# The remainder rows of a down product: one product of 96 rows, or three rounds of 32-row products in four row groups

## The chip, the cores and the metric

The kernel runs on one core of one Trainium2 chip. The metric is the device time of one execution in microseconds (us). One core has TensorE (PE, matrix products; its weight loads are listed apart as PEld), VectorE (DVE), ScalarE (ACT), GpSimd (POOL) and SyncE (SP, which here issues DMAs). Each engine works through its own instructions in order and waits on semaphores for the others.

## The reference

```python
def _B_ref(x, w_gate, w_up, w_down):
    return (_gelu(x @ w_gate) * (x @ w_up)) @ w_down
...
x = A_x
xn = _layernorm(x, axis=-1)
return x + _A_ref(xn, ...) + _B_ref(xn, B_w_gate, B_w_up, B_w_down)
```

`x` is 2048 tokens of 512 features in bfloat16. `_B_ref` is a gated feed-forward layer with an inner width of F = 1376. `_A_ref` is a state-space layer: each of 512 complex states is decayed from token to token and takes an input from a product with `B_re + iB_im`; the states are multiplied by `C_re + iC_im`, the real part doubled, and `xn * Dskip` added.

1376 = 10 x 128 + 96. The inner width is thus ten full tiles of 128 rows and a remainder of 96. This remainder is the subject here.

## The kernel before

**Blocks and stages.** The 2048 tokens are four blocks of 512 (b = 0 to 3), each of four token tiles of 128 (j). For a block there are: normalisation; a transposition to feature-major (XNT); `BU`, 32 products that give the inputs of the states, followed by `CHAIN` on VectorE (a rotation, eight scans over the 512 tokens, a rotation back) which leaves the states in SS; `GU`, the gate and up products for row tiles ft = 0 to 10 of the inner width, which after gelu on ScalarE and a multiply on VectorE leave the tile HT[b % 2][ft] (128 inner rows x 512 tokens); and `DN`, the down product, which sums in a PSUM bank, for each token tile, the products of HT with WD (11 row tiles) and of SS with CT (8 products), and puts out the sum with the skip terms.

**The down product (DN, L847 to L884).** Line 857 has the products over HT, line 865 those over SS, line 876 the product of the remainder where it is done late. Each has a token tile of 128 as its weights and 512 output features as its columns. The remainder's tile HT[.][10] holds 96 rows; it is padded with zeros to 128, as is WD's, by memsets on GpSimd at the start (L515, L516), so the remainder is one product of 128 rows per token tile. After a tile's products, `skip` (L843 to L845) prepares x + xn * Dskip on VectorE, `evO` (L881) adds it to the PSUM bank and writes OUTB, and SyncE stores it (L883).

**The remainder rows of HT.** The up products of the remainder are packed: for all blocks `GU_rest` (L801) computes the 96 gate columns and 32 of the up columns in one set of four products (L808), and `UP_rest` (L825) computes the other 64 up columns for two blocks at a time, side by side in the two column halves of the array (L832), copied out by ScalarE (L838). `h_rest` (L820, its multiply is L822) then writes the 96 rows of HT[.][10]. For blocks 0 and 1 `h_rest` can only come after `UP_rest`, for blocks 2 and 3 it comes right after `GU_rest`.

**The order.** TensorE and SyncE execute in the order in which the program is written. VectorE, ScalarE and GpSimd are ordered by a planner (`Sched.schedule`), which gives each operation a due time from that of its users and its own estimated duration; a DMA has an estimated issue time (460 ns) and latency (1900 ns). All data lie in one arena with fixed places; PSUM has 8 banks, given out in turn by `next_bank`. The end of the program's order on TensorE:

```python
        def among(free):
            BU(2, banks=free + free)
            CHAIN(2)
            for i, ft in enumerate((0, 1, 2, 3, -1, 4, 5)):
                ...
        DN(0, (0, 1, 2, 3), later=among)
        GU(2, range(6, KF))
        DN(1, (0, 1, 2, 3))
        BU(3)
        CHAIN(3)
        GU(3, [KF - 1] + list(range(KF - 1)))
        DN(2, (0, 1, 2, 3))
        DN(3, (0, 1, 2))
        DN(3, (3,), 0, 384)
        DN(3, (3,), 384, 512)
```

(In `among`, -1 stands for UP_rest, the others for gu_mm and gu_out of block 2.) With `later`, DN(0) does its ten full row tiles and the SS products of all four token tiles, then `among` on the other four banks, then the four remainder products (L876). The last token tile is split into 384 and 128 columns, so that the last store is small. Products by their lines: L719 is BU, L776 gate and up, L808 GU_rest, L832 UP_rest, L857, L865 and L876 DN. VectorE by its lines: L747, L748, L749, L752 rotations, L758 scans, L768 the last step of a chain, L788 the multiply of a full row tile. CTM is a buffer that `scale_C` uses while it makes CT; the last operations that read it end before DN(0).

Of the kernel before, what the change touches and what calls it, by code (L numbers as in the profile page):

```python
# [9 lines left out]
ALU = mybir.AluOpType  # L10
# [47 lines left out]

class Op:
    __slots__ = ("id", "eng", "fn", "dur", "deps", "kind", "reads", "writes", "prio", "start", "finish",  # L60
                 "sem", "val", "users", "tag", "slack", "silent", "pin", "issue", "lat")

    def __init__(self, id_, eng, fn, dur, kind, reads, writes, tag):
        self.id, self.eng, self.fn, self.dur, self.kind = id_, eng, fn, float(dur), kind
        self.reads, self.writes, self.tag = reads, writes, tag
        self.deps, self.users = [], []
        self.prio = 0.0
        self.start = self.finish = None
        self.sem = None
        self.val = None  # L70
        self.slack = 0.0
        self.pin = None
        self.silent = False
        self.issue, self.lat = 460.0, 1900.0


class Sched:
# [42 lines left out]
        return self._add(eng, fn, dur, "eng", reads, writes, tag, after)  # L120

    def dma(self, fn, nbytes, reads=(), writes=(), tag="", after=(), is_output=False, queue="sync", issue=460.0,
            lat=1900.0):
        op = self._add(queue, fn, lat + nbytes / 0.33e3, "dma", reads, writes, tag, after)
        op.issue, op.lat = issue, lat
        if is_output:
            self.out_ops.append(op)
        return op
# [113 lines left out]
    def emit(self):  # L242
# [8 lines left out]
        for e in ENGINES:  # L251
            for op in order[e]:
                if op.silent:
                    op.sem, op.val = None, 0
                elif op.kind == "eng":
                    cnt[e] += 1
                    op.sem, op.val = esem[e], cnt[e]
                else:
                    op.sem, op.val = es.enter_context(nc.semaphore("d%d" % nd)), 16
                    nd += 1  # L260
        self.n_sems = len(esem) + nd
        plan = {}
# [23 lines left out]
        for e in ENGINES:  # L286
            h = getattr(nc, e)
            for waits, op in plan[e]:
                for (s, v) in waits:
                    h.wait_ge(s, v)  # L290
                ins = op.fn(h)
                if not op.silent:
                    ins.then_inc(op.sem, 1 if op.kind == "eng" else 16)
        for (s, v) in final_waits:
            nc.sync.wait_ge(s, v)

# [16 lines left out]
def d_dve_tt2x(n): return 85.0 + 0.535 * n  # L313
def d_dve_1x(n): return 100.0 + 1.07 * n
# [6 lines left out]
def build(nc, ins, out):  # L321
    with ExitStack() as es:
# [111 lines left out]
        HT = ring(HT_all, "HT", 2)  # L434
        HTt = [[A.sub(HT[k], "HT%d_%d" % (k, ft), ft) for ft in range(KF)] for k in range(2)]
        CTM_all = A.alloc("CTM", [2, D], F32)
        CTM = ring(CTM_all, "CTM", 2)
        SSs = [[A.sub(SSb[k], "SS%d_%d" % (k, s), s) for s in range(KP)] for k in range(3)]
        SSc = [[[A.sub(SSs[k][s], "SS%d_%d_%d" % (k, s, c), c) for c in range(2)] for s in range(KP)] for k in range(3)]
# [61 lines left out]
        def late_loads():  # L501
# [12 lines left out]
              POOL(lambda e: e.iota(IOTJ.ap, [[1, 512]], base=0, channel_multiplier=0), 600, [], [IOTJ], "iotj"),  # L514
# [10 lines left out]
        def next_bank():  # L525
            b_ = rstate["n"] % 8
            rstate["n"] += 1
            return b_
# [156 lines left out]
        def factor():  # L685
# [16 lines left out]
            tt(CR, pa(NRE), pa(RDEN), ALU.mult, [PA[NRE], PA[RDEN]])  # L702
            tt(CI, pa(NIM), pa(RDEN), ALU.mult, [PA[NIM], PA[RDEN]])

        def scale_C():
            for s in range(KP):
                for c, (si, sr, op) in enumerate(((CI, CR, ALU.subtract), (CR, CI, ALU.add))):
                    m = CTM[c]
                    ACT(lambda e, s=s, si=si, m=m: e.activation(m.ap, CTR[1].ap[:, s, :], ACTF.Copy, scale=PA[si].ap[:, s:s + 1]),  # L709
                        d_act(512, 1), [CTR[1], PA[si]], [m], "cmul")  # L710
                    V(lambda e, s=s, sr=sr, m=m, op=op, c=c: e.scalar_tensor_tensor(  # L711
                        CT[c][s].ap, CTR[0].ap[:, s, :], PA[sr].ap[:, s:s + 1], m.ap, ALU.mult, op),
                      d_dve_1x(512), [CTR[0], PA[sr], m], [CT[c][s]], "cadd")

        def bu_mm(b, s, c, bank, c0, c1, toks):
            def f(e):
# [103 lines left out]
        def h_rest(b):  # L820
            ht = HTt[b % 2][KF - 1]
            V(lambda e: e.tensor_tensor(ht.ap[0:96, :], GGX[b % 2].ap[0:96, :], UPX[b].ap[0:96, :], ALU.mult),  # L822
              d_dve_tt2x(512), [GGX[b % 2]] + UPXp[b] + UPXj[b], [ht], "hmul")

        def UP_rest(banks):  # L825
            f0 = 128 * (KF - 1)
# [20 lines left out]
        def DN(b, js, c0=0, c1=512, later=None):  # L847
            k2, k3 = b % 2, b % 3
            banks = [next_bank() for _ in js]
            first = range(KF) if later is None else range(KF - 1)  # L850
            outs = [PS[bank][:, 0:c1 - c0] for bank in banks]
            parts = [bank_part(bank, 0, 4 * (c1 - c0)) for bank in banks]
            for j, o_, part in zip(js, outs, parts):
                def ffn(e, o_=o_, tok=slice(128 * j, 128 * (j + 1))):
                    ins_ = None
                    for ft in first:
                        ins_ = e.matmul(o_, HTt[k2][ft].ap[:, tok], WD.ap[:, ft, c0:c1], start=(ft == 0), stop=False)  # L857
                    return ins_
                PE(ffn, d_pe([c1 - c0] * len(first)), [HTt[k2][ft] for ft in first] + WDc, [part], "DN%d" % b)
            for j, o_, part in zip(js, outs, parts):  # L860
                def ssm(e, o_=o_, tok=slice(128 * j, 128 * (j + 1))):
                    ins_ = None
                    for s in range(KP):
                        for c in range(2):
                            ins_ = e.matmul(o_, SSc[k3][s][c].ap[:, tok], CT[c][s].ap[:, c0:c1], start=False,  # L865
                                            stop=(later is None and s == KP - 1 and c == 1))
                    return ins_
                PE(ssm, d_pe([c1 - c0] * 8), [SSs[k3][s] for s in range(KP)] + [CT[c][s] for c in range(2) for s in range(KP)],
                   [part], "DN%d" % b)
            if later is not None:  # L870
                later([bank for bank in range(8) if bank not in banks])
            for j, o_, part in zip(js, outs, parts):
                tt = 4 * b + j
                ko = tt % 4
                if later is not None:
                    PE(lambda e, o_=o_, tok=slice(128 * j, 128 * (j + 1)): e.matmul(  # L876
                        o_, HTt[k2][KF - 1].ap[:, tok], WD.ap[:, KF - 1, c0:c1], start=False, stop=True),
                       d_pe([c1 - c0]), [HTt[k2][KF - 1]] + WDc, [part], "DN%d" % b)
                if c0 == 0:
                    skip(tt)  # L880
                V(lambda e, o_=o_, ko=ko: e.tensor_tensor(OUTB[ko].ap[:, c0:c1], o_, XD[ko].ap[:, c0:c1], ALU.add),  # L881
                  d_dve_1x(c1 - c0), [part, XD[ko]], [out_part(ko, c0, c1)], "evO")
                S.dma(lambda e, tt=tt, ko=ko: e.dma_start(out[0, 128 * tt:128 * (tt + 1), c0:c1], OUTB[ko].ap[:, c0:c1]),  # L883
                      256 * (c1 - c0), reads=[out_part(ko, c0, c1)], is_output=True, tag="st_out")  # L884

        ONES = nc.const_aps.tensor(1.0, (128, 512), BF16)

# [89 lines left out]
        DN(3, (3,), 384, 512)  # L977

        S.schedule()
        S.emit()  # L980
# [54 lines left out]
```

## Time and profile before

| | us |
|---|---|
| median of 3 runs | 177.70 |
| lowest and highest run | 177.57, 177.71 |
| the profiled execution | 177.75 |
| its span, from the first to the last instruction | 176.4 |
| TensorE busy in it | 173.8 |
| VectorE busy | 161.2 |
| ScalarE busy | 102.4 |

The granted clock of TensorE is 1.000 on the mean over the span. Times in the views count from the start of the span. A product of 128 x 128 weights and 512 columns has a duration of 379 ns in the groups, but products overlap, so the chain of waits, which lists how long a row of them took, shows the pace. The trace lacks a few product records.

### The profile page before, as it was taken

What the parts mean: (1) busy time and instruction counts of PE and PEld (TensorE: products, weight loads), DVE (VectorE), ACT (ScalarE), POOL (GpSimd) and SP (SyncE); (2) the same over time, 40 slices, a digit from 0 to 9 for tenths busy, and PEclk for the clock granted to TensorE, in tenths of its full rate; (3) what the DMA queues carried; (4) which work ended last, traced back from release to release, by engine and by line L of the source; (5) the groups of instructions that cost most, each with busy time, mean ns of one, the idle gap of its engine ahead of it and who ended that gap; (6) DMA issues with size and microseconds to landing.
All of it is one profiled execution on the core that took longest, in us unless ns stands there. A gap on an engine that the chain in (4) does not pass through costs nothing.

```text
span 176.4 us, 2434 instructions
## 1 busy us (share of the span) xinstructions
PE 173.8 (99%) x889; PEld 82.3 (47%) x889; DVE 161.2 (91%) x251; ACT 102.4 (58%) x194; POOL 14.3 (8%) x25
## 2 busy tenths in 40 slices
PE   8999999999999999999999999999999999999995
PEld 2784444444444444444444444444444444444454
DVE  5889999998999999999899999899989999999831
ACT  3599999889999995866785700026866620000000
POOL 5130110000033019000000000000000000000000
DMA  5999825986000041230003000120000000002111
GB/s 153 252 243 342 246 59 98 320 173 186 0 0 0 4 87 33 58 61 0 4 2 119 0 0 0 35 89 0 0 0 0 4 0 0 0 0 78 45 59 59
DMA packets 26345, 12.38 MB, mean 70 GB/s; under 512 B 17662, under 2 KB 26334, under 8 KB 26334
## 3 DMA queue, kind: packets, MB, share of 16 engines
q1 hardware_dynamic: 25270, 11.71, 26.2%
q10 hardware_dynamic: 1064, 0.53, 1.0%
q8 instruction: 7, 0.11, 0.3%
q14 instruction: 4, 0.03, 0.1%
HBM read 6.46 MB, written 2.10 MB: 49 GB/s over the span
## 4 chain that ended last, share of the span: by engine, by line
PE 99%; DVE 0%; issue 0%
PE PS L776 38%; PE PS L857 21%; PE PS L865 16%; PE PS L719 16%; PE PS L892 3%; PE PS L808 2%; PE PS L613 2%; PE PS L832 1%; PE PS L589 1%; PE PS L876 0%; DVE arena L881 0%; PE PS L622 0%
## 5 line engine op out<-in xcount | busy, mean ns | idle before, releaser
L776 PE MATMUL PS<-arena 128*128 128x512 bf16 (+2 forms) x328 | 68.0, 366 | 0.0
L776 PEld LDWEIGHTS PS<-arena 128*128 128x128 bf16 x328 | 31.2, 98 | 35.2 <-ACT arena L838 0.4
L758 DVE TENSOR_TENSOR_SCAN arena<-arena 128x512 bf16<-128x512 f32 x32 | 38.4, 1252 | 0.0
L857 PE MATMUL PS<-arena 128*128 128x512 bf16 (+2 forms) x183 | 38.1, 366 | 0.0
L865 PE MATMUL PS<-arena 128*128 128x512 bf16 (+2 forms) x136 | 28.6, 366 | 0.0
L719 PE MATMUL PS<-arena 128*128 128x512 bf16 x128 | 28.3, 379 | 0.0
L784 ACT ACTIVATE arena<-PS 128x512 bf16<-128x512 f32 x40 | 23.8, 596 | 6.4 <-PE PS L776 4.9
L857 PEld LDWEIGHTS PS<-arena 128*128 128x128 bf16 x183 | 17.6, 98 | 19.9
L728 ACT ACTIVATE arena<-PS 128x512 bf16<-128x512 f32 x26 | 15.2, 600 | 19.9 <-PE PS L719 19.7
L786 ACT ACTIVATE arena<-PS 128x512 bf16<-128x512 f32 x40 | 23.9, 598 | 4.7 <-PE PS L776 4.5
L865 PEld LDWEIGHTS PS<-arena 128*128 128x128 bf16 x136 | 13.0, 98 | 14.7
L719 PEld LDWEIGHTS PS<-arena 128*128 128x128 bf16 x128 | 12.5, 98 | 14.9
L747 DVE TENSOR_TENSOR arena<-arena 128x4096 bf16<-128x4096 bf16 x8 | 18.3, 2286 | 0.1
L748 DVE TENSOR_TENSOR arena<-arena 128x4096 bf16<-128x4096 bf16 x8 | 18.3, 2284 | 0.0
L788 DVE TENSOR_TENSOR arena<-arena 128x512 bf16<-128x512 bf16 x40 | 16.0, 418 | 2.0 <-ACT arena L786 1.7
L881 DVE TENSOR_TENSOR arena<-PS,arena 128x512 bf16<-128x512 f32 (+2 forms) x17 | 10.7, 652 | 6.6 <-PE PS L865 5.8
L845 DVE TENSOR_TENSOR arena<-arena 128x512 f32<-128x512 bf16 x16 | 10.6, 689 | 0.4
L749 DVE TENSOR_TENSOR arena<-arena 128x2048 bf16<-128x2048 bf16 x8 | 9.8, 1222 | 0.2
L637 ACT ACTIVATE arena<-arena 128x512 bf16<-128x512 bf16 x8 | 5.8, 800 | 2.6 <-POOL arena L630 2.6
L534 DVE BATCH_NORM_STATS2 arena<-arena 128x6 f32<-128x512 bf16 x8 | 5.2, 680 | 1.5 <-DMA arena<-in_A_x_dram 1.4
L844 DVE TENSOR_TENSOR arena<-arena 128x512 bf16<-128x512 bf16 x16 | 6.3, 418 | 0.0
L711 DVE SCALAR_TENSOR_TENSOR arena<-arena 128x512 bf16<-128x512 bf16 x8 | 5.7, 747 | 0.5 <-ACT arena L709 0.5
(78 smaller groups left out, 113.3 us busy)
## 6 DMA issues: line engine op xcount, KB each, us to landing
out_dram<-arena SPq DMA_DIRECT2D x15, 128.0 KB, 1.7
arena<-in_A_x_dram SPq DMA_DIRECT2D x3, 512.0 KB, 6.8
arena<-in_B_w_down_dram SPq DMA_DIRECT2D x1, 1280.0 KB, 7.7
arena<-in_B_w_gate_dram SPq DMA_DIRECT2D x2, 384.0 KB, 6.5
arena<-in_B_w_up_dram SPq DMA_DIRECT2D x2, 384.0 KB, 7.0
arena<-in_A_x_dram SPq DMA_DIRECT2D x4, 128.0 KB, 3.1
arena<-in_B_w_gate_dram ACTq DMA_DIRECT2D x1, 256.0 KB, 3.2
arena<-in_B_w_up_dram ACTq DMA_DIRECT2D x1, 256.0 KB, 4.0
```

The lines of the kernel that those rows point to most:

```text
L719: ins_ = e.matmul(PS[bank][:, c0:c1], BBT[c].ap[:, dk, 128 * s:128 * (s + 1)], XNT[b].ap[:, dk, c0:c1], start=(dk == 0), stop=(dk == KD - 1))
L728: return ACT(lambda e: e.activation(ss.ap, PS[bank][:, :], ACTF.Copy), d_act(512), [BANK[bank]], [ss], "evBu", slack=1500.0)
L747: V(lambda e: e.tensor_tensor(TB.ap, ssb.ap, sin4, ALU.mult), d_dve_tt2x(4096), [ssb, SINT], [TB], tag, after=GATE["rot"])
L748: V(lambda e: e.tensor_tensor(TA.ap, ssb.ap, cos4, ALU.mult), d_dve_tt2x(4096), [ssb, COST], [TA], tag, after=GATE["rot"])
L758: V(lambda e, g=g, rb=rb, init=init: e.tensor_tensor_scan(g.ap, rb, g.ap, init, ALU.mult, ALU.add), d_dve_scan(512), [g, PA[RRr]] + ([CARc ...
L776: ins_ = e.matmul(PS[bank][0:m, c0:c1], W.ap[:, dk, 128 * ft:128 * ft + m], XNT[b].ap[:, dk, c0:c1], start=(dk == 0), stop=(dk == KD - 1))
L784: g = ACT(lambda e: e.activation(GG[kk].ap[0:m, :], PS[bg][0:m, :], ACTF.Gelu_apprx_tanh), d_act(512), [BANK[bg]], [GG[kk]], "gelu", after ...
L786: u = ACT(lambda e: e.activation(UPB[kk].ap[0:m, :], PS[bu][0:m, :], ACTF.Copy), d_act(512), [BANK[bu]], [UPB[kk]], "evU", slack=1500.0)
L788: h = V(lambda e: e.tensor_tensor(HTt[k2][ft].ap[0:m, :], GG[kk].ap[0:m, :], UPB[kk].ap[0:m, :], ALU.mult), d_dve_tt2x(512), [GG[kk], UPB[ ...
L857: ins_ = e.matmul(o_, HTt[k2][ft].ap[:, tok], WD.ap[:, ft, c0:c1], start=(ft == 0), stop=False)
L865: ins_ = e.matmul(o_, SSc[k3][s][c].ap[:, tok], CT[c][s].ap[:, c0:c1], start=False, stop=(later is None and s == KP - 1 and c == 1))
L881: V(lambda e, o_=o_, ko=ko: e.tensor_tensor(OUTB[ko].ap[:, c0:c1], o_, XD[ko].ap[:, c0:c1], ALU.add), d_dve_1x(c1 - c0), [part, XD[ko]], [ ...
```

## The change

**What it does.** The remainder of 96 rows is cut into three pieces of 32 rows. A product of 32 rows uses one of the array's four row groups, and the four row groups are given the four token tiles of a block. For this each row group needs its own copy of the weights' rows and its own token tile's rows on its own partitions:

- WDR holds the 96 rows of `w_down`'s remainder as three pieces of 32 rows, four times, once for each group of 32 partitions. `wd_spread` loads it with 4 DMAs. It lies in the place of CTM, so it waits for CTM's last readers.
- HTR[0] and HTR[1] hold the remainder rows of HT for a block (block b uses b % 2): group g has token tile g, three pieces of 32 rows. `h_spread`, called at the end of `h_rest`, fills it with 12 DMAs from HT, arena to arena, on SyncE's queue.
- `rest_mm` does 12 products for a block: for each of the three pieces, the four row groups, each into its own PSUM bank.

Down products are written out with `ffn_mm` (products over HT), `ssm_mm` (over SS), `rest_mm` and `dn_out` in place of `DN`. The remainders of two blocks are put next to each other: blocks 0 and 1 after `among` and the first five row tiles of block 1; blocks 2 and 3 after the first four row tiles of block 3. So DN(1) comes ahead of the rest of GU(2) and not behind it, and the outputs of block 2 come after the first four row tiles of block 3. The 128-column piece of the last token tile keeps all eleven row tiles in the old form, with 96 rows. The padding of HT and WD and its memsets go. A DMA operation may now have several parts on one semaphore (`parts`).

```diff
+        WDR = A.alloc("WDR", [3, D], BF16, at=CTM_all.lo)
+        WDRb = Buf("WDRb", "wdr", 0, 1)
+        HTR = [A.alloc("HTR0", [3, 128], BF16, at=CTM_all.lo + 3072), A.alloc("HTR1", [3, 128], BF16)]
+        HTRb = [Buf("HTRb%d" % k, "htr", k, k + 1) for k in range(2)]
...
-              POOL(lambda e: e.memset(WD.ap[:, KF - 1, :], 0.0), 300, [], [WDc[1]], "pad"),
-              *[POOL(lambda e, k=k: e.memset(HT[k].ap[:, KF - 1, :], 0.0), 300, [], [HTt[k][KF - 1]], "pad")
-                for k in range(2)])
...
               d_dve_tt2x(512), [GGX[b % 2]] + UPXp[b] + UPXj[b], [ht], "hmul")
+            h_spread(b)
+
+        def h_spread(b):
+            k2 = b % 2
+            ht = HTt[k2][KF - 1]
+            S.dma(lambda e: [e.dma_start(HTR[k2].ap[32 * g:32 * g + 32, i, :], ht.ap[32 * i:32 * i + 32, 128 * g:128 * g + 128])
+                             for g in range(4) for i in range(3)],
+                  96 * 1024, reads=[ht], writes=[HTRb[k2]], tag="st_htr", after=CTMW if k2 == 0 else [], issue=1500.0, parts=12)
+
+        def wd_spread():
+            S.dma(lambda e: [e.dma_start(WDR.ap[32 * g:32 * g + 32], ins["B_w_down"][1280:F, :].rearrange("(i p) d -> p i d", p=32))
+                             for g in range(4)],
+                  4 * 96 * 1024, reads=[], writes=[WDRb], tag="ld_wdr", after=CTMW, parts=4)
...
+        def rest_mm(b, banks, stop, cols=(512,) * 4):
+            k2 = b % 2
+
+            def f(e):
+                ins_ = None
+                for i in range(3):
+                    for g in range(4):
+                        rows = slice(32 * g, 32 * g + 32)
+                        ins_ = e.matmul(PS[banks[g]][:, 0:cols[g]], HTR[k2].ap[rows, i, :], WDR.ap[rows, i, 0:cols[g]], start=False,
+                                        stop=(stop and i == 2))
+                return ins_
+            PE(f, d_pe([512] * 3) + 40, [WDRb, HTRb[k2]], [bank_part(banks[g], 0, 4 * cols[g]) for g in range(4)], "DN%d" % b)
...
-        DN(0, (0, 1, 2, 3), later=among)
+        T4, MOST = range(4), range(KF - 1)
+        wd_spread()
+        b0 = [next_bank() for _ in T4]
+        for j in T4:
+            ffn_mm(0, j, b0[j], MOST)
+        for j in T4:
+            ssm_mm(0, j, b0[j], stop=False)
+        free = [bank for bank in range(8) if bank not in b0]
+        among(free)
+        b1 = free[2:] + free[:2]
+        for j in T4:
+            ffn_mm(1, j, b1[j], range(5))
+        rest_mm(0, b0, True)
+        rest_mm(1, b1, False)
+        for j in T4:
+            dn_out(0, j, b0[j])
+        for j in T4:
+            ffn_mm(1, j, b1[j], range(5, KF - 1))
+        for j in T4:
+            ssm_mm(1, j, b1[j])
+            dn_out(1, j, b1[j])
+        rstate["n"] = b0[0]
         GU(2, range(6, KF))
-        DN(1, (0, 1, 2, 3))
         BU(3)
         CHAIN(3)
         GU(3, [KF - 1] + list(range(KF - 1)))
-        DN(2, (0, 1, 2, 3))
-        DN(3, (0, 1, 2))
-        DN(3, (3,), 0, 384)
-        DN(3, (3,), 384, 512)
+        b2 = [next_bank() for _ in T4]
+        b3 = [next_bank() for _ in T4]
+        for j in T4:
+            ffn_mm(2, j, b2[j], MOST)
+        for j in T4:
+            ssm_mm(2, j, b2[j], stop=False)
+        WIDE = (512, 512, 512, 384)
+        for j in T4:
+            ffn_mm(3, j, b3[j], range(4), 0, WIDE[j])
+        rest_mm(2, b2, True)
+        rest_mm(3, b3, False, WIDE)
+        for j in T4:
+            dn_out(2, j, b2[j])
+        for j in T4:
+            ffn_mm(3, j, b3[j], range(4, KF - 1), 0, WIDE[j])
+        for j in T4:
+            ssm_mm(3, j, b3[j], 0, WIDE[j])
+            dn_out(3, j, b3[j], 0, WIDE[j])
+        ffn_mm(3, 3, b2[0], range(KF), 384, 512)
+        ssm_mm(3, 3, b2[0], 384, 512)
+        dn_out(3, 3, b2[0], 384, 512)
```

More of the change, by code (lines that the diff above doesn't have):

```diff
@@ L60 @@
     __slots__ = ("id", "eng", "fn", "dur", "deps", "kind", "reads", "writes", "prio", "start", "finish",
-                 "sem", "val", "users", "tag", "slack", "silent", "pin", "issue", "lat")
+                 "sem", "val", "users", "tag", "slack", "silent", "pin", "issue", "lat", "parts")
     def __init__(self, id_, eng, fn, dur, kind, reads, writes, tag):
@@ L73, in __init__ @@
         self.silent = False
-        self.issue, self.lat = 460.0, 1900.0
+        self.issue, self.lat, self.parts = 460.0, 1900.0, 1
 class Sched:
@@ L122, in dma @@
     def dma(self, fn, nbytes, reads=(), writes=(), tag="", after=(), is_output=False, queue="sync", issue=460.0,
-            lat=1900.0):
+            lat=1900.0, parts=1):
         op = self._add(queue, fn, lat + nbytes / 0.33e3, "dma", reads, writes, tag, after)
-        op.issue, op.lat = issue, lat
+        op.issue, op.lat, op.parts = issue, lat, parts
         if is_output:
@@ L258, in emit @@
                 else:
-                    op.sem, op.val = es.enter_context(nc.semaphore("d%d" % nd)), 16
+                    op.sem, op.val = es.enter_context(nc.semaphore("d%d" % nd)), 16 * op.parts
                     nd += 1
@@ L292, in emit @@
                 if not op.silent:
-                    ins.then_inc(op.sem, 1 if op.kind == "eng" else 16)
+                    for one in ins if op.parts > 1 else (ins,):
+                        one.then_inc(op.sem, 1 if op.kind == "eng" else 16)
         for (s, v) in final_waits:
@@ L513, in build @@
               POOL(lambda e: e.memset(EB4.ap, math.e), 100, [], [EB4], "const"),
-              POOL(lambda e: e.iota(IOTJ.ap, [[1, 512]], base=0, channel_multiplier=0), 600, [], [IOTJ], "iotj"),
-              POOL(lambda e: e.memset(WD.ap[:, KF - 1, :], 0.0), 300, [], [WDc[1]], "pad"),
-              *[POOL(lambda e, k=k: e.memset(HT[k].ap[:, KF - 1, :], 0.0), 300, [], [HTt[k][KF - 1]], "pad")
-                for k in range(2)])
+              POOL(lambda e: e.iota(IOTJ.ap, [[1, 512]], base=0, channel_multiplier=0), 600, [], [IOTJ], "iotj"))
         S.pin(V(lambda e: e.memset(PRMT.ap[32:64, :], 0.0), D_TINY, [], PRM[3:4], "pad"),
@@ L703, in factor @@
             tt(CI, pa(NIM), pa(RDEN), ALU.mult, [PA[NIM], PA[RDEN]])
+        CTMW = []
         def scale_C():
@@ L710, in scale_C @@
                         d_act(512, 1), [CTR[1], PA[si]], [m], "cmul")
-                    V(lambda e, s=s, sr=sr, m=m, op=op, c=c: e.scalar_tensor_tensor(
+                    cv = V(lambda e, s=s, sr=sr, m=m, op=op, c=c: e.scalar_tensor_tensor(
                         CT[c][s].ap, CTR[0].ap[:, s, :], PA[sr].ap[:, s:s + 1], m.ap, ALU.mult, op),
                       d_dve_1x(512), [CTR[0], PA[sr], m], [CT[c][s]], "cadd")
+                    CTMW[c:] = [cv]
         def bu_mm(b, s, c, bank, c0, c1, toks):
@@ L845, in skip @@
             V(lambda e: e.tensor_tensor(XD[tt % 4].ap, X[tt].ap, XN[tt].ap, ALU.add), d_dve_1x(512), [X[tt], XN[tt]], [XD[tt % 4]], "xd")
[L847 to L884, printed above, removed]
@@ new lines, in ffn_mm @@
+        def ffn_mm(b, j, bank, fts, c0=0, c1=512):
+            k2, tok = b % 2, slice(128 * j, 128 * (j + 1))
+            def f(e):
+                ins_ = None
+                for ft in fts:
+                    m = FROWS[ft]
+                    ins_ = e.matmul(PS[bank][:, 0:c1 - c0], HTt[k2][ft].ap[0:m, tok], WD.ap[0:m, ft, c0:c1], start=(ft == 0), stop=False)
+                return ins_
+            PE(f, d_pe([c1 - c0] * len(fts)), [HTt[k2][ft] for ft in fts] + [WDc[ft // 10] for ft in fts],
+               [bank_part(bank, 0, 4 * (c1 - c0))], "DN%d" % b)
@@ new lines, in ssm_mm, with f @@
+        def ssm_mm(b, j, bank, c0=0, c1=512, stop=True):
+            k3, tok = b % 3, slice(128 * j, 128 * (j + 1))
+            def f(e):
+                ins_ = None
+                for s in range(KP):
+                    for c in range(2):
+                        ins_ = e.matmul(PS[bank][:, 0:c1 - c0], SSc[k3][s][c].ap[:, tok], CT[c][s].ap[:, c0:c1], start=False,
+                                        stop=(stop and s == KP - 1 and c == 1))
+                return ins_
+            PE(f, d_pe([c1 - c0] * 8), [SSs[k3][s] for s in range(KP)] + [CT[c][s] for c in range(2) for s in range(KP)],
+               [bank_part(bank, 0, 4 * (c1 - c0))], "DN%d" % b)
@@ new lines, in rest_mm, with f @@
+        def rest_mm(b, banks, stop, cols=(512,) * 4):
+            k2 = b % 2
+            def f(e):
+                ins_ = None
+                for i in range(3):
[3 more added lines that the diff above has]
+                                        stop=(stop and i == 2))
+                return ins_
+            PE(f, d_pe([512] * 3) + 40, [WDRb, HTRb[k2]], [bank_part(banks[g], 0, 4 * cols[g]) for g in range(4)], "DN%d" % b)
@@ new lines, in dn_out @@
+        def dn_out(b, j, bank, c0=0, c1=512):
+            tt, ko = 4 * b + j, j
+            if c0 == 0:
+                skip(tt)
+            V(lambda e: e.tensor_tensor(OUTB[ko].ap[:, c0:c1], PS[bank][:, 0:c1 - c0], XD[ko].ap[:, c0:c1], ALU.add),
+              d_dve_1x(c1 - c0), [bank_part(bank, 0, 4 * (c1 - c0)), XD[ko]], [out_part(ko, c0, c1)], "evO")
+            S.dma(lambda e: e.dma_start(out[0, 128 * tt:128 * (tt + 1), c0:c1], OUTB[ko].ap[:, c0:c1]),
+                  256 * (c1 - c0), reads=[out_part(ko, c0, c1)], is_output=True, tag="st_out")
```

## The prediction, made before the changed kernel was run

> **What bounds the kernel now.** I read the page's busy times first, then the chain of work that ended last as pieces in order of time, then the timelines of VectorE and SyncE around the place that the change touches.
>
> ```profile
> span 176.4 us, 2434 instructions
> ...
> PE 173.8 (99%) x889; PEld 82.3 (47%) x889; DVE 161.2 (91%) x251; ACT 102.4 (58%) x194; POOL 14.3 (8%) x25
> ```
>
> TensorE is busy for 99% of the span, and the chain is TensorE for 99% too. The pieces of the chain show how densely:
>
> ```profile
> 86.20 1.85 PE PS L832 x16
> 88.05 3.56 PE PS L776 x16
> 91.61 0.86 PE PS L876 x4
> 92.48 6.91 PE PS L776 x32
> ...
> 170.39 1.79 PE PS L857 x11
> ...
> 173.48 0.61 PE PS L857 x11
> ```
>
> Columns: start, length, what, how many products. 6.91 / 32 = 0.216 us for a product of 512 columns; 1.79 / 11 = 0.163 us for 384 columns; 0.61 / 11 = 0.056 us for 128. Each piece starts where the one before it ends, so nothing is waited for. Hence two rules: a product less is worth 0.216 us at the end, and any time for which TensorE has to wait is added to the end in full, since no idle stretch is there to take it up. VectorE has slack late: its timeline ends the last scan chain's work (L768) at 156.1, and the products that read it (the last L865 pieces) begin at 165.2.
>
> **The products.** Removed: the remainder of 96 rows costs one product for each of 16 token tiles. The 128-column piece of the last tile keeps its own (all 11 row tiles stay in it), so 15 x 0.216 + 0.163 = 3.40 us go. Added: 12 products of 32 rows for each block, four of them meant to run at once in four row groups: 3 rounds x 0.216 = 0.65 us a block, 2.59 us for four, if the four really run side by side. All other products keep their number and their shape.
>
> The trace has no row groups, but it has the column halves of L832: 16 products of 64 output rows, two at a time, in 1.85 us, where 8 x 0.216 = 1.73. So two share the array fully, and one excursion into the divided array costs 0.12 us for going in and out. The change makes two such excursions (blocks 0 and 1 together, 2 and 3 together): 2.59 + 0.24 = 2.83 us, 0.71 for each of a pair. I take that value, as L832 is the nearest row. Bounds: 2.59 (no cost at the borders) and 48 x 0.216 = 10.4 (no overlap at all). The weight loads, four in a round: the 128-column products above, each with a load of its own, follow each other every 0.056 us, so four loads need 0.22 us, which just fits under a round. Products alone: 2.83 - 3.40 = **-0.57 us**.
>
> The Trainium skill, "TensorE: Matmul & The Clock Gate", section "Measured speedup vs the span model", states 3.07 times for four row tiles of 32 rows and 512 columns, not 4 times; no trace here shows that shape. By it the rounds would take 48 x 0.216 / 3.07 = 3.38 us (an estimate from that page), and the products' saving would be gone: 0.8 us more than my sum.
>
> **The wait that is added.** A remainder product now reads HTR, which 12 DMAs for each block fill from HT (h_spread), all issued by SyncE. For blocks 0 and 1 these can't start before the last rows of HT exist, and those come from the up products of L832, right before:
>
> ```profile
> 85.49 2.28 DVE L748 TENSOR_TENSOR arena<-arena 128x4096 bf16<-128x4096 bf16 x1
> 87.85 0.42 DVE L822 TENSOR_TENSOR arena<-arena 96x512 bf16<-96x512 bf16 x1
> 88.20 0.42 DVE L788 TENSOR_TENSOR arena<-arena 128x512 bf16<-128x512 bf16 x1
> 88.53 0.41 DVE L822 TENSOR_TENSOR arena<-arena 96x512 bf16<-96x512 bf16 x1
> ```
>
> The two L822 are block 0's and block 1's. The first ends at 88.27; ScalarE's copy that it needs (L838) starts at 87.23 and takes 0.59, so it can hardly be earlier. What follows is SyncE's time per DMA:
>
> ```profile
> 0.72 0.88 SPq L455 DMA_DIRECT2D arena<-in_A_x_dram  x2
> 1.64 0.37 SPq L473 DMA_DIRECT2D arena<-in_A_Lambda_re_dram  x1
> 2.06 0.83 SPq L455 DMA_DIRECT2D arena<-in_A_x_dram  x2
> 2.93 0.90 SPq L473 DMA_DIRECT2D arena<-in_A_Lambda_im_dram  x1
> ```
>
> Back-to-back issues start every 0.42 to 0.46 us (0.72 to 1.64 is two; 1.64 to 2.06 is one, of 4 short rows: few rows make it hardly cheaper). Stores out of the arena are the cheapest:
>
> ```profile
> L883 SPq DMA_DIRECT2D out_dram<-arena x17: 332/332/362, 93.0 to 174.9; - x17
> ...
> DMA to landing us min/median/max: 1.4/1.7/1.9
> ```
>
> 0.33 us each, with the gaps of about 0.045 seen between issues 0.375 from start to start. The planner counts 1500 ns for all twelve; the trace says 12 x 0.375 to 12 x 0.46, 4.5 to 5.5 us, three times that or more, and the queue is in order: block 1's twelve stand behind block 0's. I take 0.40 (between the store row and the 4-row load, 32 rows of 256 bytes being like both). Landing: 1.7, the median of the stores; bounds 1.4 (their fastest) and 2.5, the only row from arena to arena:
>
> ```profile
> arena<-arena SPq DMA_TRANSPOSE x12, 2.5
> ```
>
> Start of the issues: 88.27 + 0.08 (the first evO ends at 92.96, its store is issued at 93.00; a little for the hand-over). VectorE's order is planned anew, and the planner now counts about 2 us between L822 and its use where it had none, so I allow one 0.42 us multiply ahead of it (bounds 0, and 1.2 for one L749). The last of 24 issues starts 23 x 0.40 = 9.2 later, and lands 1.7 after: 88.27 + 0.08 + 0.42 + 9.2 + 1.7 = **99.7**. Bounds: 88.35 + 8.6 + 1.4 = 98.4, and 88.35 + 1.2 + 10.6 + 2.5 = 102.6.
>
> TensorE comes there sooner. It leaves the products of L776 at 91.61, as before; then 20 products of block 1 (5 row tiles x 4) take 4.32, to 95.93. Block 0's twelve landed at 88.8 + 11 x 0.40 + 1.7 = 94.9, so its remainder runs without a wait, to 96.64. Block 1's then waits until 99.7: **3.0 us** of idle TensorE (bounds 1.7 and 6.0). Queued behind the waiting product are 20 products and 32 scan products of block 1, then everything else; all of them wait with it. Nothing gives that time back, as no other idle stretch exists.
>
> **What is hidden.** The second pair, blocks 2 and 3: L822 of block 3 ends at 135.3 before, some 10 us later now at the most; 24 issues and a landing add 11.3, to 157, and its products come after DN2's 72 and DN3's first 16 (about 163). No wait. wd_spread's four loads come in SyncE's queue behind the eight transposes that end at 76.95, take about 2 us and land near 81: hidden by 15 us; had they no cover, 4 us. Block 0's stores stand behind block 1's spread and go out at about 98 instead of 93; the next writer of OUTB is block 1's evO after 106, so nobody waits. Block 1's scan products (L865) come some 5 us earlier than at 109.74, at 104.7; their chain (L768) ends at 92.4 and covers it. VectorE's evO of block 2 comes later, at about 165; with 4 evO (2.5) and the 4 pairs of L844 and L845 (4.0) behind them VectorE is just ready for block 3's first evO, near 171.7. The three memsets that go (1.6 us on an engine busy 8%) cost nothing. The tail of 19 products of 128 columns, evO and store is the same.
>
> **Sum**, against the profiled execution: 177.75 us, 1.35 around its span of 176.4; the median of the runs, 177.70, is 0.05 lower. 177.75 - 0.57 + 3.03 = **180.2 us**.
>
> **The rivals.**
> - *No wait (other side, faster).* SyncE issues these small DMAs faster than any row shows. The point from which it decides: the wait must be under 0.57, so the last landing before 97.2, which is an issue every 0.29 us with 1.7 for landing. At the planner's 0.125 there is no wait and 177.2 remains. Against it: the shortest record is 0.33 even without its gap. Chance 0.09; another 0.05 for a wait that just balances the saving, at 177.7.
> - *The idle stretch cools the clock.* At the start, after idling, the first ten products (L892, nine of 512 columns and one of 256) take 4.21 us on the chain, where 9.5 x 0.216 = 2.05, though the granted clock reads 1.000 on the mean. Such a spell again costs 2.1 us: 182.3. For it: the wait of 3.0 us is far longer than any of TensorE's in this trace; nothing in the trace gives the length that triggers it. Chance 0.13. The Trainium skill, "TensorE: Matmul & The Clock Gate", section "What's actually happening", puts the clock's window at about 3.4 us of idle, near the upper half of my bounds; no run here shows it.
> - *The row groups don't run side by side.* 10.4 us for the 48 products; the first remainder then covers 1.9 of the wait, 177.75 + 7.0 + 1.1 = 185.8. Against it: the column halves of L832 do run together. Chance 0.06.
> - *VectorE's new order comes out late* (a 2.3 us L747 ahead of L822, or evO of two blocks ahead of a multiply that ScalarE waits for): another 2.3, 182.5. Chance 0.05.
>
> **Chances and range.** The forecast has 0.62, about 180.2 (178.9 to 183.1 by the bounds of the wait). With the cooled clock the range 178.8 to 183.0 holds about 8 in 10; outside lie the no-wait cases and the row groups in sequence. 0.2% is 0.36 us, about what measurements of this kernel tell from no change. Faster by more: 0.09, the no-wait case; within: 0.05; slower: 0.86, all the others.
>
> **What would show it.** In the changed profile: the second remainder group (12 products) starts at about 99.7, 3 us after the first, and is released by a DMA from arena to arena; SyncE shows 24 issues in a row from 88.4, 0.38 to 0.46 apart; near 163 two remainder groups stand together in about 1.4 us. I am wrong if the issues lie closer than 0.29 apart, if the second group starts right behind the first, if a remainder takes more than 0.9 us, or if TensorE idles elsewhere.

## The result and the profile after

The changed kernel takes 187.34 us (median of 5 runs, 187.04 to 187.73) against 177.61 for the kernel before: the ratio is 1.0533, with a 95% interval of 1.0516 to 1.0551. It is 9.7 us slower; the forecast was 2.5 us slower. The profiled execution took 187.16 us, with a span of 185.9.

The page of the changed kernel, its busy times, the granted clock in 40 slices and the first line of the chain that ended last:

```profile
span 185.9 us, 2550 instructions
...
PE 175.3 (94%) x921; PEld 81.9 (44%) x921; DVE 160.8 (87%) x251; ACT 102.5 (55%) x194; POOL 11.6 (6%) x22
...
PEclk9999999999999999999999589999999999999999
...
PE 89%; SPq 7%; DMA 1%; ACT 1%; issue 1%; DVE 0%
```

TensorE is at 94% where it had 99%. The clock row, which the page of before doesn't have, shows two slices of 4.6 us below full speed. The chain is no longer TensorE alone: 7% of it is SyncE's queue. The timeline of TensorE around the first pair of remainders (L873 is block 1's row tiles, L900 the remainder products):

```profile
91.49 4.48 PE L873 MATMUL PS<-arena 128*128 128x512 bf16 x20
97.24 0.83 PE L900 MATMUL PS<-arena 32*128 32x512 bf16 x12 [1.27 <-DMA arena<-arena]
104.78 1.47 PE L900 MATMUL PS<-arena 32*128 32x512 bf16 x12 [6.71 <-DMA arena<-arena]
106.18 5.43 PE L873 MATMUL PS<-arena 128*128 128x512 bf16 x20
```

In brackets stands how long the engine idled before, and for what. TensorE waits 1.27 us for block 0's rows and 6.71 for block 1's, both for DMAs from arena to arena. After the second wait the same 12 products take 1.47 us instead of 0.83, and the 20 products 5.43 instead of 4.48. The chain between, in order of time:

```profile
88.98 0.04 issue
89.03 0.58 SPq L835
89.61 0.04 issue
89.65 0.59 SPq L835
...
102.27 0.04 issue
102.32 0.59 SPq L835
102.91 0.04 issue
102.95 1.78 DMA arena<-arena
```

It is an unbroken row of issues, 0.63 us from start to start, and one landing of 1.78. The line of the 48 issues, and below it their landing times:

```profile
L835 SPq DMA_DIRECT2D arena<-arena x48: 507/590/1251, 88.3 to 154.6; - x48
...
DMA to landing us min/median/max: 1.7/1.8/2.9
```

Median 590 ns for an issue of 32 rows of 256 bytes; the stores of the kernel before took 332. The granted clock is read from the table by windows (length, busy time of each engine with the number of instructions, then PEclk):

```profile
core 0: us, PE busy (x) PEld busy (x) DVE busy (x) ACT busy (x) POOL busy (x), PEclk, DMA share, GB/s
100.00:101.00 1.00, 0.00 (x0) 0.00 (x0) 1.00 (x3) 0.00 (x0) 0.00 (x0) 1.00 0.04 8
101.00:102.00 1.00, 0.00 (x0) 0.00 (x0) 1.00 (x3) 0.00 (x0) 0.00 (x0) 0.65 0.08 17
...
107.00:108.00 1.00, 1.00 (x4) 0.44 (x3) 0.00 (x0) 0.00 (x0) 0.00 (x0) 0.50 0.00 0
108.00:109.00 1.00, 1.00 (x6) 0.40 (x5) 0.00 (x0) 0.00 (x0) 0.00 (x0) 0.94 0.00 0
```

0.65 in a window of 1 us is full speed for 0.3 and half for 0.7: the clock halves at 101.3, some 3.2 us into the wait, and comes back at 108.1, 6.8 us later. Only the part after 104.78 costs: 1.47 - 0.76 for the remainder (0.76 is what 12 such products take at full clock, below) and 106.25 to 111.6 instead of 4.32 for the 20 products, 0.7 + 1.0 = 1.7 us.

The difference between the two profiled executions, 187.16 - 177.75 = 9.4 us, is then: waits 8.0, slow clock 1.7, products saved 0.4 (below), sum 9.3.

### The profile page after: what moved, and what is told of

Same layout as the page of the kernel before. It is cut to its first block, busy times and chain, and to the rows that moved or that the text cites. A ratio compares the mean times of both kernels' runs of the same rounds, so it can differ in the third digit from the quotient of the medians.

```text
span 185.9 us, 2550 instructions
## 1 busy us (share of the span) xinstructions
PE 175.3 (94%) x921; PEld 81.9 (44%) x921; DVE 160.8 (87%) x251; ACT 102.5 (55%) x194; POOL 11.6 (6%) x22
## 4 chain that ended last, share of the span: by engine, by line
PE 89%; SPq 7%; DMA 1%; ACT 1%; issue 1%; DVE 0%
PE PS L781 34%; PE PS L873 17%; PE PS L885 15%; PE PS L724 15%; SPq L835 7%; PE PS L920 2%; PE PS L813 2%; PE PS L900 2%; PE PS L615 2%; DMA arena<-arena 1%; PE PS L591 1%; ACT arena L857 1%; PE PS L851 1%; DVE arena L827 0%; DVE arena L909 0%
## 5 line engine op out<-in xcount | busy, mean ns | idle before, releaser
L781 PE MATMUL PS<-arena 128*128 128x512 bf16 (+2 forms) x328 | 68.0, 366 | 0.0
L781 PEld LDWEIGHTS PS<-arena 128*128 128x128 bf16 x328 | 31.1, 98 | 35.3 <-ACT arena L857 0.4
L873 PE MATMUL PS<-arena 128*128 128x512 bf16 (+2 forms) x171 | 36.7, 372 | 0.0
L885 PE MATMUL PS<-arena 128*128 128x512 bf16 (+2 forms) x136 | 28.5, 367 | 0.0
L873 PEld LDWEIGHTS PS<-arena 128*128 128x128 bf16 x171 | 16.4, 99 | 20.2 <-issue 2.6
L885 PEld LDWEIGHTS PS<-arena 128*128 128x128 bf16 x136 | 13.0, 97 | 14.7
L724 PEld LDWEIGHTS PS<-arena 128*128 128x128 bf16 x128 | 12.5, 98 | 14.9
L793 DVE TENSOR_TENSOR arena<-arena 128x512 bf16<-128x512 bf16 x40 | 15.9, 413 | 2.2 <-ACT arena L791 1.9
L900 PE MATMUL PS<-arena 32*128 32x512 bf16 (+1 forms) x48 | 3.8, 434 | 8.0 <-DMA arena<-arena 8.0
```

The source lines that it names most:

```text
L724: ins_ = e.matmul(PS[bank][:, c0:c1], BBT[c].ap[:, dk, 128 * s:128 * (s + 1)], XNT[b].ap[:, dk, c0:c1], start=(dk == 0), stop=(dk == KD - 1))
L781: ins_ = e.matmul(PS[bank][0:m, c0:c1], W.ap[:, dk, 128 * ft:128 * ft + m], XNT[b].ap[:, dk, c0:c1], start=(dk == 0), stop=(dk == KD - 1))
L793: h = V(lambda e: e.tensor_tensor(HTt[k2][ft].ap[0:m, :], GG[kk].ap[0:m, :], UPB[kk].ap[0:m, :], ALU.mult), d_dve_tt2x(512), [GG[kk], UPB[ ...
L873: ins_ = e.matmul(PS[bank][:, 0:c1 - c0], HTt[k2][ft].ap[0:m, tok], WD.ap[0:m, ft, c0:c1], start=(ft == 0), stop=False)
L885: ins_ = e.matmul(PS[bank][:, 0:c1 - c0], SSc[k3][s][c].ap[:, tok], CT[c][s].ap[:, c0:c1], start=False, stop=(stop and s == KP - 1 and c = ...
```

## The experiments

Theory A: the whole loss is TensorE's wait for the spread's landings, set by SyncE's time for each issue, and the slow clock that the wait brings. Rival B: the issue's price goes by its rows, so that fewer, larger DMAs would not help. Rival C: the row-group products or the new order cost something themselves. Each run was compared with the kernel before on the same chip.

| kernel | issues of the first pair | wait before the second remainder | us | kernel before | ratio, 95% interval |
|---|---|---|---|---|---|
| e2_four | 8 | none | 177.44 | 177.84 | 0.9979 [0.9965, 0.9993] |
| e5_later2 | 24 | none | 177.46 | 177.77 | 0.9981 [0.9972, 0.9990] |
| e6_apart | 8 | none | 177.64 | 177.77 | 0.9995 [0.9982, 1.0007] |
| e3_pool | 12 and 12 | none (1.3 before the first) | 178.90 | 177.84 | 1.0061 [1.0046, 1.0076] |
| e9_dose14 | 14 | 1.9 | 179.58 | 177.75 | 1.0104 [1.0087, 1.0121] |
| e7_dose | 15 | 2.6 | 181.79 | 177.77 | 1.020 [1.015, 1.025] |
| e4_eight | 16 | 3.2 | 182.25 | 177.84 | 1.024 [1.0202, 1.0278] |
| e1_later | 36 | see below | 183.83 | 177.84 | 1.0345 [1.0314, 1.0376] |
| e8_dram | 24 | 3.8 | 184.56 | 177.77 | one run |
| e10_fill | 24 | filled with products | 185.77 | 177.75 | 1.0469 [1.0429, 1.0508] |

### Fewer DMAs: e2_four

The edit, shortened to the source and the destination of each DMA:

```diff
-e.dma_start(HTR[k2].ap[32 * g:32 * g + 32, i, :], ht.ap[32 * i:32 * i + 32, 128 * g:128 * g + 128])
-    for g in range(4) for i in range(3)
+e.dma_start(HTR[k2].ap[32 * g:32 * g + 32], ht.ap[0:96, 128 * g:128 * g + 128])
+    for g in range(4)
-WDR: ins["B_w_down"][1280:F, :].rearrange("(i p) d -> p i d", p=32)
+WDR: ins["B_w_down"][1280:F, :].rearrange("(p i) d -> p i d", i=3)
```

One DMA for each row group carries all 96 rows: row 3p + i goes to partition p, piece i, which is the source's own order, so the destination is 32 rows of 768 bytes.

> Order as in the changed kernel, but a block's spread is 4 DMAs of 96 rows instead of 12 of 32 (the remainder's rows are dealt to the pieces as 3p+i instead of 32i+p, in WDR too). Theory A with a price for each DMA (0.63 from issue to issue whatever its rows): last landing 88.35 + 7 x 0.633 + 1.8 = 94.6, before TensorE's 95.9, no wait, 177.1. Rival B (the price goes by the rows, 0.63 for 32): an issue takes 1.9, last landing 88.35 + 7 x 1.9 + 1.8 = 103.5, a wait of 7 us and the slow clock, 185 to 186.

Measured: 177.44 us, no wait. Its issues and its TensorE timeline:

```profile
L836 SPq DMA_DIRECT2D arena<-arena x16: 562/597/705, 88.8 to 137.6; - x16
```

```profile
91.92 4.48 PE L875 MATMUL PS<-arena 128*128 128x512 bf16 x20
96.33 1.47 PE L902 MATMUL PS<-arena 32*128 32x512 bf16 x24
97.97 4.26 PE L875 MATMUL PS<-arena 128*128 128x512 bf16 x19 [0.16 <-DVE arena L911]
```

Three times the rows, and an issue still takes 597 ns. Rival B falls: the price is per DMA. Both remainders (24 products) start as soon as the 20 products before them are through. The 0.16 named after VectorE is no wait: one of the 20 L875 records is missing there.

### More of them, and the length of the wait: e4_eight, e7_dose, e9_dose14

```diff
+ns = [(2, 2, 2, 2), (2, 2, 2, 1)][k2]
+e.dma_start(HTR[k2].ap[32 * g + 32 // n * q:32 * g + 32 // n * (q + 1)],
+            ht.ap[96 // n * q:96 // n * (q + 1), 128 * g:128 * g + 128])
+    for g, n in enumerate(ns) for q in range(n)
```

`ns` is the number of DMAs for each row group, for block 0 and block 1; shown is e7_dose. In e4_eight block 1 has (2, 2, 2, 2) too, in e9_dose14 (2, 2, 1, 1).

> As e2_four, but 8 DMAs of 48 rows for each block. Theory A with a price for each DMA: last landing 88.35 + 15 x 0.633 + 1.8 = 99.6, TensorE there at 96.6, a wait of 3.0 us; that is just under the 3.3 us of idling after which the clock fell in the changed kernel, so if the clock goes by the length of the idle time it stays at 1.00 and the time is 177.1 + 3.0 = 180.1; if any long wait halves it, 181.8. Rival B (price by rows): about 185 to 186, as for the changed kernel.

> 15 DMAs for the first pair (8 for block 0, 7 for block 1, of 48 rows, one of 96): last landing 88.35 + 14 x 0.633 + 1.85 = 99.1, TensorE there at 96.6, a wait of 2.4 us, between the 1.3 after which the clock stayed and the 3.2 after which it fell. If the clock falls after it: 177.2 + 2.4 + 1.7 = 181.3; if not: 179.6.

> 14 DMAs for the first pair (8 and 6): last landing 88.3 + 13 x 0.635 + 1.85 = 98.4, TensorE there at 96.6, a wait of 1.9 us. After 2.6 and 3.2 us three executions of four had a mean clock of 0.991 and were 1.4 to 1.7 us longer than the fourth with 1.000. If the drop depends on how much of a fixed window of the clock's the wait covers, shorter waits meet it less often: 179.3 in most executions, at most a few at 180.9. If every wait over some length drops it: all at 180.9, or none.

Measured, the second remainder of e4_eight, e7_dose and e9_dose14, from the timelines of TensorE:

```profile
99.87 1.11 PE L902 MATMUL PS<-arena 32*128 32x512 bf16 x12 [3.16 <-DMA arena<-arena]
```

```profile
99.21 0.83 PE L902 MATMUL PS<-arena 32*128 32x512 bf16 x12 [2.56 <-DMA arena<-arena]
```

```profile
98.55 0.83 PE L902 MATMUL PS<-arena 32*128 32x512 bf16 x12 [1.92 <-DMA arena<-arena]
```

The waits are what 0.63 for each issue gives: one issue more is 0.60 to 0.64 us more wait. The expectation for e4_eight had left the clock open, and both of its cases occurred: three of the four executions have a mean clock of 0.991 and take 182.2 to 182.7 us, the fourth 1.000 and 181.0. In e7_dose three have 0.991 and 181.7 to 182.0, the fourth 1.000 and 180.24. In e9_dose14 all four have 1.000 (179.35 to 179.69). So a wait of 1.9 us did not bring the slow clock in four executions, 2.6 and 3.2 did in three of four each, at a price of 1.2 to 1.7 us, and 6.7 did in all five of the changed kernel. In the profiled executions of e4_eight and e7_dose the clock falls only after the products run again (at 100.3 and 100.1), and both times stays down for 3.4 us.

### The remainders later: e1_later and e5_later2

Both leave the 24 DMAs of 32 rows and put other products ahead of the first pair of remainders. The diff is e5_later2's; in e1_later `GU_rest(2)` stands ahead of the `ffn_mm` loop.

```diff
         among(free)
+        for i, ft in enumerate(range(6, KF - 1)):
+            bg, bu = free[2 - 2 * (i % 2)], free[3 - 2 * (i % 2)]
+            gu_mm(2, ft, bg, bu)
+            gu_out(2, ft, bg, bu)
...
         for j in T4:
-            ffn_mm(1, j, b1[j], range(5))
+            ffn_mm(1, j, b1[j], MOST)
         rest_mm(0, b0, True)
         rest_mm(1, b1, False)
...
         for j in T4:
-            ffn_mm(1, j, b1[j], range(5, KF - 1))
-        for j in T4:
             ssm_mm(1, j, b1[j])
             dn_out(1, j, b1[j])
         rstate["n"] = b0[0]
-        GU(2, range(6, KF))
+        GU_rest(2)
```

> The spread stays as it is (24 DMAs, 0.633 us from issue to issue, last landing near 104.7), but the two remainders of blocks 0 and 1 come later on TensorE: the rest of block 2's gate and up products (36 products, 7.8 us) and all ten row tiles of block 1 (40 products, 8.6 us) stand ahead of them, so TensorE comes there at 91.5 + 16.4 = 107.9. Theory A (the loss is TensorE's wait for the landings, 8.2 us, and the slow clock after it, 1.7 us, and nothing else): no wait, granted clock 1.00, 177.75 - 0.6 = 177.1. Rival C (the row-group products or the new order on VectorE cost something of their own): no wait either, but 178 or more.

Measured: 183.83 us, and a wait. The edit was at fault: GU_rest(2) spreads block 2's rows, and written ahead of block 0's remainder product it makes that product read block 2's rows, so the layer isn't computed as in the reference. TensorE waited for 36 DMAs, not 24: 88.45 + 35 x 0.633 + 1.8 = 112.4, and the first remainder starts at 112.54. It says nothing on rival C, but it confirms the queue's arithmetic.

> The changed kernel with its 24 DMAs of 32 rows, but with four row tiles of block 2's gate and up products (32 products, 6.9 us) and all ten row tiles of block 1 (40, 8.6 us) ahead of the first pair of remainders, and block 2's own remainder rows behind them. TensorE comes there at 91.5 + 15.5 = 107.0, the last landing is near 104.7. Theory A (the loss is the wait and the slow clock): no wait, clock 1.00, 177.75 - 0.5 = 177.2. Rival C (row groups or the new order cost something themselves): 178 or more without a wait.

Measured: 177.46 us. Its TensorE timeline, L873 block 1's row tiles, L885 its scan products:

```profile
98.28 8.80 PE L873 MATMUL PS<-arena 128*128 128x512 bf16 x39
107.01 1.47 PE L900 MATMUL PS<-arena 32*128 32x512 bf16 x24
108.64 6.85 PE L885 MATMUL PS<-arena 128*128 128x512 bf16 x31 [0.16 <-DVE arena L909]
```

The 24 issues and the landing times are those of the changed kernel, and with the wait gone the loss is gone: 9.9 us less, by the order alone. Rival C falls. Like e2_four it is faster than the kernel before, by 0.2%.

### The other queue: e3_pool

```diff
-S.dma(..., parts=12)
+S.dma(..., parts=12, queue="gpsimd" if b == 1 else "sync")
```

> The changed kernel with block 1's twelve DMAs issued from GpSimd's queue instead of SyncE's, so that both blocks' issues run beside each other. Theory A: block 0's still land at 88.35 + 11 x 0.633 + 1.8 = 97.1, a wait of 1.3 us; block 1's decide by GpSimd's time per DMA, which no run has shown: at 0.63 it adds nothing more, 178.4; at 1.0 they land near 88.9 + 11 + 1.8 = 101.7, a wait of 5 in all and the slow clock, 183 to 184. If SyncE's queue were not the cause, the time would stay at 187.

Measured: 178.90 us; one wait of 1.30 us before the first remainder, none before the second, clock 1.000 in all runs. GpSimd's twelve in its timeline:

```profile
89.56 6.12 POOL L835 DMA_DIRECT2D arena<-arena  x12 [18.73 <-DVE arena L827]
```

6.12 / 12 = 0.51 us each. With two queues side by side the block 1 rows are there before block 0's.

### One pair apart: e6_apart

```diff
+        rest_mm(2, b2, True)
         for j in T4:
             ffn_mm(3, j, b3[j], range(4), 0, WIDE[j])
-        rest_mm(2, b2, True)
         rest_mm(3, b3, False, WIDE)
```

> The kernel with 4 DMAs for each block, but block 2's remainder stands right behind its own scan products and block 3's where it was, so the second pair is two excursions into row groups instead of one. Theory A: each group takes 0.65 + 0.1 at its borders, 0.1 more in all than the pair's 1.40: 177.5. Rival (going in and out is what costs): 0.4 or more.

Measured: 177.64 us. Its chain at the end:

```profile
157.17 0.76 PE PS L902 x12
157.93 3.35 PE PS L875 x16
161.28 0.76 PE PS L902 x9
```

The 12 products of block 2's remainder take 0.76 us (0.65 are three rounds of 0.216), but the way out of the row groups shows only in the piece behind them. Its 16 products (12 of 512 columns, 4 of 384) take 3.35, where their pace is 12 x 0.216 + 4 x 0.163 = 3.24. In e2_four, where no remainder stands right ahead of them, they do take that:

```profile
157.48 3.24 PE PS L875 x16
```

So a remainder by itself costs 0.76 + 0.11 = 0.87. Of block 3's remainder three records are missing; the 18 products of 512 columns and 6 of 384 behind it end at 167.00, which puts their start at 167.00 - 18 x 0.216 - 6 x 0.163 = 162.13, and the remainder at 162.13 - 161.28 = 0.85. Apart the two cost 1.72. For the pair, the chain of e2_four has the first one start at 96.40 and the 20 products behind it end at 102.23; 20 x 0.216 before that is 97.91, so a pair takes 1.51. (Its second pair starts at 160.72, and the same 24 products behind it end at 167.09, which gives 1.51 too.) "Two blocks at one place" is thus worth 0.2 us here, more than the 0.1 expected and less than the rival's 0.4. The timed runs of the two kernels differ by 0.2 as well, though their intervals overlap. Each excursion into the row groups costs about 0.2 at its borders, with 12 products (0.87 - 0.65) as with 24 (1.51 - 1.30).

### Where the issue's price comes from: e8_dram

```diff
-ht.ap[32 * i:32 * i + 32, 128 * g:128 * g + 128]
+ins["B_w_down"][1280 + 32 * i:1312 + 32 * i, 128 * g:128 * g + 128]
```

> The changed kernel, but its 24 DMAs of 32 rows of 256 bytes fetch rows of w_down from DRAM instead of HT's rows (the remainder's product is then not the layer's; all else is left). If the price of an issue depends on the way (arena to arena 0.59, DRAM to arena 0.43): 0.47 from issue to issue, last landing 88.35 + 23 x 0.47 + 2.2 = 101.4, a wait of 4.7 in all and a slow spell, 183. If it depends on the small rows: 0.63 and 187 as in the changed kernel.

Measured: 184.56 us; a wait of 3.84 us before the second remainder, none before the first, clock 0.981. Its issues:

```profile
L835 SPq DMA_DIRECT2D arena<-in_B_w_down_dram x48: 310/421/1092, 88.6 to 148.3; - x48
```

The same shape from DRAM takes 421 ns, 10.99 us for 24, or 0.46 from start to start. This is one run, but the four loads of `wd_spread` in the changed kernel, from DRAM too, have a median of 430 ns. With the shape held, the source alone thus makes the difference of 0.17. The run is 1.5 us over the expected 183, although its wait is shorter than expected: the clock is half from 100.1 to 106.9, twice as long as after the waits of 2.6 and 3.2. TensorE works from 100.80 on, so 6.1 us of work go at half speed, which costs some 3 us.

### The wait filled with products: e10_fill

```diff
         rest_mm(0, b0, True)
+        for j in T4:
+            dn_out(0, j, b0[j])
+        warm_pe(26, 512, b0[0])
         rest_mm(1, b1, False)
-        for j in T4:
-            dn_out(0, j, b0[j])
```

> The changed kernel with its 24 DMAs, but 26 products of the constant ones (5.6 us, into a bank of block 0 that is already read out) stand between the two remainders of the first pair, where TensorE would idle 6.7 us; they add work and leave the landing at 104.7. Theory A: clock 1.00 throughout, and the time falls by the slow spell alone, 1.7 us: 185.6. Rival (the time after the wait is slow for another reason, for example the row-group products or the landings): 187.3 or more.

Measured: 185.77 us (185.68 to 185.78 in three executions with a clock of 1.000; 187.18 in one with 0.991).

```profile
98.92 5.86 PE L920 MATMUL PS<-const-bfloat16-1.0 128*128 128x512 bf16 x25 [0.80 <-DVE arena L909]
104.84 0.83 PE L900 MATMUL PS<-arena 32*128 32x512 bf16 x12
105.60 4.49 PE L873 MATMUL PS<-arena 128*128 128x512 bf16 x19
```

(`dn_out(0)` moves up because the added products overwrite one of block 0's banks. One record each of L920 and L873 is missing.) The second remainder starts at 104.84 as before (104.78), but now runs in 0.83 instead of 1.47, and the products behind it in 4.49 instead of 5.43: work that is good for nothing saves 1.6 us. The slow clock's share is thus measured by itself.

## Why the prediction was wrong, point by point

**Direction and mechanism: right.** Block 1's remainder waits for the last of 24 DMAs in SyncE's queue, and what it waits for is lost at the end. e5_later2 and e2_four, which take away only the wait, leave no loss.

**The step that failed: 0.40 us for each issue.** The prediction took 0.40 "between the store row and the 4-row load", with bounds of 0.375 and 0.46. It measured 0.633. All its rows had DRAM at one end, and it reasoned from the number of rows; e4_eight and e2_four show that the rows don't matter (32, 48 and 96 rows: 590, 592 and 597 ns) and e8_dram that the source does: from DRAM the same DMAs go every 0.46, the prediction's upper bound. 23 x (0.633 - 0.40) = 5.4 us: the forecast landing, 99.7, becomes 105.1, and 104.78 was measured. The upper bound, 102.6, was made of the wrong range as well: a row from arena to arena was in the trace, the transposes, and gave only the landing time there. Their issue time in SyncE's timeline (the first four take 5.13 us, 1.3 each) lay above all bounds taken. The range of 0.42 to 0.46 also left out a row of the fence that it was read from: the single load of Lambda_im, 0.90.

**The sum of the miss.** The profiled execution is 7.0 us over the forecast of 180.2. Of it 5.0 are the wait (8.0 and not 3.0), 1.7 the slow clock, which was not in the sum, and 0.2 the products; 0.1 is left.

**Landing, start.** 1.7 forecast, 1.78 measured. The issues start at 88.35, as worked out; the 0.42 allowed for a new order on VectorE did not occur.

**Block 0's remainder** was to run without a wait (landing 94.9); it waited 1.3 us, by the same term (11 x 0.233 = 2.6 us later).

**The clock**, a rival with a chance of 0.13 at 2.1 us, came with the longer wait and cost 1.7. The Trainium skill, "TensorE: Matmul & The Clock Gate", section "What's actually happening", puts the throttle at a full idle window of about 3.4 us. The runs agree on the length: the slow spells last 3.4 us (e4_eight, e7_dose) or 6.8 (the changed kernel, e8_dram). They differ on the idle time needed: 2.6 us was enough in three executions of four. What a spell costs depends on how much of it falls on work: 1.2 to 1.7 us in e4_eight and e7_dose, some 3 in e8_dram.

**The products.** Forecast 2.83 us for all 48, measured 1.51 for a pair, 3.02, so the saving is 3.40 - 3.02 = 0.38 and not 0.57; e2_four and e5_later2, 0.40 and 0.31 us below the kernel before, bear it out. The borders cost about 0.2 a pair (1.51 less six rounds of 0.216), not 0.12. The prediction took its 0.12 from the line of L832 alone, and the way out of the divided array stands in the next line of its fence: 3.56 us for 16 products, 0.10 above 16 x 0.216 = 3.46, close to the 0.11 behind the remainder of e6_apart. With 0.22 for each excursion its sum is 2.59 + 0.44 = 3.03. Four row groups do run side by side: 12 products in 0.76 us, where in sequence they would take 2.59. The Trainium skill, "TensorE: Matmul & The Clock Gate", section "Measured speedup vs the span model", has 3.07 times for four row tiles; borders included, it is 12 x 0.216 / 0.87 = 3.0 here for a remainder by itself and 24 x 0.216 / 1.51 = 3.4 for a pair.

**What was to be hidden** was: no wait for wd_spread or for the second pair, where TensorE goes from 16 products of block 3 straight into both remainders, and none for VectorE's late evO.

## What to carry to other kernels

Before a step is fed by many small DMAs, multiply their number by the issue time of the same way (here 0.63 us from arena to arena on one queue), and add one landing; compare that with when the consumer gets there. Where the sum is late, put fewer and larger DMAs, a second queue, or other work ahead of the consumer: each of the three took the 8 us away or nearly so. On an engine without idle time a wait costs its length, and waits of 2.6 us and more brought a slow clock as well in most executions here.

## What the runs showed of the hardware that was not expected

- A small DMA took SyncE 0.59 us to issue from arena to arena, whether it had 32, 48 or 96 rows of 256 bytes, and 0.42 from DRAM with 32 such rows. The stores, of another shape, took 0.33. These are not prices for every DMA: the single loads at the start of the kernel before took 0.37 to 1.89. On GpSimd's queue the DMA of 32 rows from arena to arena took 0.51 from start to start. Why the source matters no run here shows.
- TensorE's clock can fall after the idle time that causes it: in e7_dose 0.9 us after the products ran again. Whether a wait of 2.6 to 3.2 us brings it differed from execution to execution of one program (three of four). That would fit a clock that is decided at moments of its own and not after a fixed length of idle time, but no run here sets those moments, so it stays a reading.
- In e10_fill one execution of four had the slow clock although the longest idle stretches seen in the profiled one are 1.4 and 0.8 us, with 0.83 us of products between them; what brought it there is open.
